# An FFT mixing and relu-squared feed-forward kernel: the first block by eight plain products, w_out's sums moved to VectorE, another order of roundings and G

## The chip, the cores and the metric

One core of a Trainium2 chip. The time is device microseconds of the whole program, the median of several runs. The profile's span (first to last instruction) is about 1.8 us shorter than the time. Engines: TensorE (PE, its weight loads PEld), VectorE (DVE), ScalarE (ACT), GpSimd (POOL); SP issues the transfers.

## The reference, cut to what matters

```python
x: (8, 3008, 256)                      # batch, sequence, width; float32
X = np.fft.fft(np.fft.fft(x, axis=1), axis=2).real        # attention part
h = X.reshape(24064, 256) @ w_in       # w_in (256, 2048), float64 in memory
g = np.maximum(h, 0.0) ** 2
out = g @ w_out                        # w_out (2048, 256), float64 in memory
```

## The kernel before: the parts that matter

The two transforms never appear as such. Of the sequence transform three small arrays P, Q and E are made (cosine and sine sums, in groups called `dft_ops` with table products `pd` and VectorE's joins); the transform over the width is multiplied into w_in once, which gives G1, G2 and gE. A **step** then handles 128 columns of w_in twice (j and j + 8) for 251 frequencies. Eight steps are a block, six blocks a batch of the sequence, eight batches the whole: 384 steps.

```python
def front(b, k0, n, j, between):       # 4 products, 6 VectorE instructions
    for h in range(2):
        ...
        nc.tensor.matmul(hP, G1[:, fs], pt[:, ks], ...)             # ph
        nc.tensor.matmul(hQ, G2[:, fs], qt[:, ks], ...)             # ph
        nc.vector.scalar_tensor_tensor(out=t, in0=et[:, ks], ... in1=hP, ...)   # he
        tt(out=g[:, h, 0, 0:n], in0=t, in1=hQ, op=ALU.add)
        tt(out=g[:, h, 1, 0:n][:, ::-1], in0=t, in1=hQ, op=ALU.subtract)
        between()                      # a piece of the next batch's transform
def combine(n, g):                     # ScalarE, then GpSimd
    act(v, v, AF.Relu); act(v, v, AF.Square)
    gt(out=s1, ...); gt(out=s2, ...); gt(out=s3, ...); gt(out=s4, ...)
def back(n, j, g, s, final):           # 7 products with sums in place of 8
    products = [("mA", 0, wout[:, j, 0, 0], g[:, 0, 0]), ... ("mD", 0, wout[:, j, 1, 1], s[:, 3])]
```

The seven products are a Strassen scheme: they need four sums of g in every step (GpSimd) and, once, four sums of w_out's quarters.

The first block has a second task. The weights lie in memory as 64-bit floats and are rounded by hand, one piece (128 x 512) at a time: two VectorE instructions and three on ScalarE start it, three on VectorE end it.

```python
def convert(dst, src):
    ...                                                  # transfer of the raw words
    nc.vector.tensor_scalar(out=eb, in0=high, ...)       # start: exponent bits
    act(e, eb, AF.Relu, ...); act(eb, e, AF.Relu, ...)
    nc.vector.tensor_scalar(out=mb, in0=high, ...)       # start: mantissa bits
    act(rest, low, AF.Copy, scale=2.0 ** -32)
    def finish():                                        # end
        nc.vector.scalar_tensor_tensor(out=eb, ...)
        tt(out=m, in0=mb, in1=rest, op=ALU.add)
        nc.vector.scalar_tensor_tensor(out=dst, in0=pairs(m), ..., in1=pairs(e), ...)
    return finish
def load_win(j):  ... finish(); then G1, G2, gE of j: products pg, pe and three ScalarE copies
def load_wout(j): ... finish(); then four GpSimd sums of w_out's quarters
...
for i in range(len(steps) + LAG + 4):                    # LAG = 2
    if i < NJ:
        for _ in range(2 if i + 2 < NJ else 1):
            next_weight()              # starts one piece, ends the one started before it
    g = front(b, k0, n, j, between)
    ... back() of step i - 2 ...
    flight.append(((b, k0, n, j), g, combine(n, g)))
```

## Time and profile before

| | before |
|---|---|
| time, median of 3 (range) | 2010.53 us (2009.85 to 2014.74) |
| span of the profiled run, granted clock | 2008.3 us, 0.990 |
| TensorE busy | 1959.6 us |
| first `ph` / first `he` | 67.79 / 69.16 us |
| `ph` of step 8 (second block) | 132.28 us |
| first `ph` of batch 1 | 341.55 us |

How to read it: TensorE is the bound, so only its idle time can be won without taking products away. The three marks in the last rows cut the run into pieces that can be compared one by one: the transform of batch 0, the first block, the rest of batch 0 (210 us), and seven batches that the change does not touch. One more line, from who waited for whom between 60 and 120 us (total, number, longest, in us):

```profile
PE pg L236 <- DVE win L220: 17.3, 6, 4.5
```

All waits of TensorE in that stretch are of this one kind, for the last instruction of a rounding of w_in.

### The profile page before, as it was taken

How to read it: one execution, taken by the hardware profiler on the slowest of the kernel's cores; microseconds unless marked ns; L12 is line 12 of the kernel's file. 1: busy time of each engine (PE TensorE's matmuls, PEld its weight loads, DVE VectorE, ACT ScalarE, POOL GpSimd, SP SyncE). 2: the span in 40 equal slices, each digit the busy share in tenths (PEclk: the TensorE clock that was granted, in tenths of full speed). 3: DMA queues.
4: the chain of work that ended last, by engine and by line, in shares of the span. 5: the costliest groups of instructions: out<-in, count | busy, mean ns of one | idle time of the engine just before them, and what ended most of it. 6: DMA issues, size and time to landing. Idle time of an engine off the chain costs nothing.

```text
span 2008.3 us, 27310 instructions
## 1 busy us (share of the span) xinstructions
PE 1959.6 (98%) x9088; PEld 1702.4 (85%) x9088; DVE 1395.1 (69%) x3463; ACT 897.9 (45%) x973; POOL 1199.8 (60%) x1763
## 2 busy tenths in 40 slices
PE   5799999999999999999999999999999999999998
PEld 3578888888888888888888888888888888888887
DVE  6899766877577765787557875687757776555554
ACT  1554444444444544444444444444444444444443
POOL 0366655766566665666556665566656675556664
PEclk8899999999999999999999999999999999999999
DMA  6223101110011101111011110111001100100100
GB/s 182 85 63 61 30 11 32 35 44 22 11 37 47 27 22 30 33 31 43 16 26 37 35 33 11 31 38 41 22 11 40 44 11 16 31 11 11 21 11 21
DMA packets 144687, 68.49 MB, mean 34 GB/s; under 512 B 128440, under 2 KB 135547, under 8 KB 144546
## 3 DMA queue, kind: packets, MB, share of 16 engines
q1 hardware_dynamic: 143470, 66.24, 14.1%
q8 instruction: 71, 1.16, 0.2%
q10 hardware_dynamic: 1076, 0.52, 0.1%
q14 instruction: 70, 0.57, 0.1%
HBM read 42.03 MB, written 24.68 MB: 33 GB/s over the span
## 4 chain that ended last, share of the span: by engine, by line
PE 95%; DVE 3%; DMA 1%; issue 0%; ACT 0%; SPq 0%; DVEq 0%
PE ph L413 16%; PE mA L456 16%; PE mC L456 16%; PE ph L414 16%; PE mB L456 16%; PE mD L456 8%; PE pd L353 5%; PE pg L236 1%; DMA xt<-in_x_dram 1%; DVE he L416 0%; DMA raw<-in_moe_w_in_dram 0%; DVE fd L217 0%; DVE fs L219 0%; DVE g L419 0%; DVE win L220 0%
## 5 line engine op out<-in xcount | busy, mean ns | idle before, releaser
L427 ACT ACTIVATE g<-g 128x1004 f32<-128x1004 f32 (+1 forms) x384 | 399.5, 1040 | 883.0 <-DVE g L419 506.1
L416 DVE SCALAR_TENSOR_TENSOR he<-Et,gE,ph 128x251 f32<-128x251 f32 (+1 forms) x768 | 361.7, 471 | 480.9 <-PE ph L414 479.5
L433 POOL TENSOR_TENSOR s<-g 128x251 f32<-128x251 f32 (+1 forms) x384 | 253.4, 660 | 629.2 <-ACT g L428 569.1
L413 PE MATMUL ph<-Pt,G 128*128 128x251 f32 (+1 forms) x1536 | 452.6, 375 | 0.9 <-DVE g L419 0.9
L414 PE MATMUL ph<-Qt,G 127*128 127x251 f32 (+1 forms) x1536 | 451.2, 374 | 0.0
L428 ACT ACTIVATE g<-g 128x1004 f32<-128x1004 f32 (+1 forms) x384 | 399.3, 1040 | 12.2
L456 PE MATMUL mA<-g,wout 128*128 128x251 f32 (+1 forms) x1536 | 389.5, 375 | 0.0
L456 PE MATMUL mC<-s,wsum 128*128 128x251 f32 (+1 forms) x1536 | 389.3, 374 | 0.0
L418 DVE TENSOR_TENSOR g<-he,ph 128x251 f32<-128x251 f32 (+1 forms) x768 | 320.6, 417 | 56.0 <-ACT g L428 0.5
L456 PEld LDWEIGHTS mA<-g,wout 128*128 128x128 f32 x1536 | 288.3, 189 | 43.5 <-issue 4.0
L413 PEld LDWEIGHTS ph<-Pt,G 128*128 128x128 f32 x1536 | 287.7, 189 | 42.9 <-issue 3.2
L414 PEld LDWEIGHTS ph<-Qt,G 127*128 127x128 f32 x1536 | 291.2, 190 | 35.8
L456 PEld LDWEIGHTS mC<-s,wsum 128*128 128x128 f32 x1536 | 291.6, 190 | 35.2
L419 DVE TENSOR_TENSOR g<-he,ph 128x251 f32<-128x251 f32 (+1 forms) x768 | 314.1, 409 | 0.0
L434 POOL TENSOR_TENSOR s<-s,g 128x251 f32<-128x251 f32 (+1 forms) x384 | 286.8, 747 | 30.1
L435 POOL TENSOR_TENSOR s<-g 128x251 f32<-128x251 f32 (+1 forms) x384 | 298.1, 776 | 0.0
L436 POOL TENSOR_TENSOR s<-g,s 128x251 f32<-128x251 f32 (+1 forms) x384 | 252.4, 657 | 0.0
L456 PE MATMUL mB<-g,wsum 128*128 128x251 f32 (+1 forms) x768 | 225.1, 374 | 0.0
L456 PE MATMUL mD<-s,wout 128*128 128x251 f32 (+1 forms) x768 | 225.0, 374 | 0.0
L456 PE MATMUL mB<-s,wout 128*128 128x251 f32 (+1 forms) x768 | 224.6, 374 | 0.0
L456 PEld LDWEIGHTS mB<-g,wsum 128*128 128x128 f32 x768 | 145.6, 190 | 17.7
L456 PEld LDWEIGHTS mD<-s,wout 128*128 128x128 f32 x768 | 144.9, 189 | 18.1
(79 smaller groups left out, 1239.9 us busy)
## 6 DMA issues: line engine op xcount, KB each, us to landing
out_dram<-os SPq DMA_DIRECT2D x376, 56.0 KB
xt<-in_x_dram SPq DMA_DIRECT2D x24, 512.0 KB
xt<-in_x_dram SPq DMA_DIRECT2D x16, 384.0 KB
Et<-e_dram SPq DMA_DIRECT2D x7, 752.5 KB
out_dram<-os SPq DMA_DIRECT2D x288, 6.8 KB
raw<-in_moe_w_in_dram SPq DMA_DIRECT2D x16, 256.0 KB
raw<-in_moe_w_out_dram SPq DMA_DIRECT2D x16, 256.0 KB
xt<-in_x_dram SPq DMA_DIRECT2D x8, 480.0 KB
```

The lines of the kernel that those rows point to most:

```text
L413: nc.tensor.matmul(hP, G1[:, fs], pt[:, ks], start=True, stop=True)
L414: nc.tensor.matmul(hQ, G2[:, fs], qt[:, ks], start=True, stop=True)
L416: nc.vector.scalar_tensor_tensor(out=t, in0=et[:, ks], scalar=gE[:, fc:fc + 1], in1=hP, op0=ALU.mult, op1=ALU.add)
L418: tt(out=g[:, h, 0, 0:n], in0=t, in1=hQ, op=ALU.add)
L419: tt(out=g[:, h, 1, 0:n][:, ::-1], in0=t, in1=hQ, op=ALU.subtract)
L427: act(v, v, AF.Relu)
L428: act(v, v, AF.Square)
L433: gt(out=s1, in0=g21, in1=g22, op=ALU.add)
L434: gt(out=s2, in0=s1, in1=g11, op=ALU.subtract)
L435: gt(out=s3, in0=g11, in1=g21, op=ALU.subtract)
L436: gt(out=s4, in0=g12, in1=s2, op=ALU.subtract)
L456: nc.tensor.matmul(acc[nm][:, i, 0:n], w, v[:, 0:n], start=j == 0 and i == 0, stop=j == NJ - 1, skip_group_check=True)
```

## The change

Its intent is to start the steady state earlier. The first block does without sums (eight plain products), so GpSimd is silent while VectorE rounds; w_out's sums are made by VectorE in the second block, when the roundings are over; batch 0's side work starts a block later to leave room for that; G's products are issued a step after their rounding; w_out is rounded before w_in; a rounding is put into a wait in Q's transform; and w_out's halves are separated by reading every second element, not by writing apart.

```diff
-    def pairs(w):
-        return w.rearrange("p c (e h) -> p (c e) h", h=2)
+    def parts(w, k):
+        return w.rearrange("p c (e h) -> p h (c e)", h=k)
...
-            gt = nc.gpsimd.tensor_tensor
-            gt(out=t3, in0=b22, in1=b12, op=ALU.subtract)
+    def sum_wout(j):
+        tt(out=t3, in0=b22, in1=b12, op=ALU.subtract)
...                                              # and three more sums
-    def combine(n, g):
+    def combine(n, g, plain):
...
+        if plain:
+            return None
...
+        if s is None:
+            for c in range(2):
+                for h in range(2):
+                    for side, nm in enumerate(("mA", "mB")):
+                        nc.tensor.matmul(acc[nm][:, h, 0:n], wout[:, j, h, c], g[:, c, side, 0:n], ...)
...
+        weights.append(lambda j=j: load_wout(j))
         if j + 2 < NJ:
             weights.append(lambda j=j: load_win(j + 2))
-        weights.append(lambda j=j: load_wout(j))
...
+    groups_at(20, 25)
     begun = weights.pop(0)()
-    groups_at(16, 20, 17, 18, 19, 21, 22, 23)
-    next_weight()
+    groups_at(21, 22, 23)
+    products = next_weight()
+    groups_at(26, 27, 28, 24, 29)
+    products = [products]
...
-        if i < NJ:
+        if i < 2 * NJ:                           # no side work yet
             return
...
-            if i < NJ:
-                for _ in range(2 if i + 2 < NJ else 1):
-                    next_weight()
...
             g = front(b, k0, n, j, between)
+            if i < NJ:
+                s = combine(n, g, True)
+            elif i < 2 * NJ:
+                sum_wout(j)
...                                              # back() of step i - 2
+        for f in products:
+            f()
+        products = [next_weight() for _ in range(2 if i + 2 < NJ else 1 if i < NJ else 0)]
```

More of the change, by code (lines that the diff above doesn't have):

```diff
@@ L180, in pair_out @@
         return moe_w_out.rearrange("(c j p) (o e) -> j c p o e", j=NJ, p=P, o=1)[j]
-    def pairs(w):
-        return w.rearrange("p c (e h) -> p (c e) h", h=2)
+    def parts(w, k):
+        return w.rearrange("p c (e h) -> p h (c e)", h=k)
     raws = 0
     def convert(dst, src):
+        k = dst.shape[1]
         nonlocal raws
@@ L194, in convert @@
                 nc.sync.dma_start(out=w[:, c].rearrange("p (o e) -> p o e", o=src.shape[2]), in_=src[c])
-            return lambda: nc.vector.tensor_copy(dst, pairs(w))
+            return lambda: nc.vector.tensor_copy(dst, parts(w, k))
         pool, tag = (xp, "x") if raws % (NX + 1) else (ep, "c")
@@ L219, in finish @@
             tt(out=m, in0=mb, in1=rest, op=ALU.add)
-            nc.vector.scalar_tensor_tensor(out=dst, in0=pairs(m), scalar=2.0 ** -20, in1=pairs(e),
+            nc.vector.scalar_tensor_tensor(out=dst, in0=parts(m, k), scalar=2.0 ** -20, in1=parts(e, k),
                                            op0=ALU.mult, op1=ALU.mult)
@@ L228, in load_win, with products @@
         w = ep.tile([P, 2, CH], F32, name="win", tag="sB" if j % 2 else "sA")
-        finish = convert(pairs(w), pair_in(j))
-        def then():
-            finish()
+        finish = convert(parts(w, 1), pair_in(j))
+        def products():
             for tab, G, n in ((cosd, G1, P), (sind, G2, P - 1)):
@@ L244, in then @@
             nc.scalar.copy(gE[:, j::NJ], ps[:, 0:2])
-        return then
+        return finish, products
     def load_wout(j):
-        finish = convert(wout[:, j].rearrange("p h c e -> p (c e) h"), pair_out(j))
-        def then():
-            finish()
-            b11, b12, b21, b22 = (wout[:, j, h, c] for c in range(2) for h in range(2))
-            t2, t3, t4 = (wsum[:, i, j] for i in range(3))
-            gt = nc.gpsimd.tensor_tensor
-            gt(out=t3, in0=b22, in1=b12, op=ALU.subtract)
-            gt(out=b12, in0=b12, in1=b11, op=ALU.subtract)
-            gt(out=t2, in0=b22, in1=b12, op=ALU.subtract)
-            gt(out=t4, in0=t2, in1=b21, op=ALU.subtract)
-        return then
+        return convert(wout[:, j].rearrange("p h c e -> p h (c e)"), pair_out(j)), lambda: None
+    def sum_wout(j):
+        b11, b12, b21, b22 = (wout[:, j, h, c] for c in range(2) for h in range(2))
+        t2, t3, t4 = (wsum[:, i, j] for i in range(3))
+        tt(out=t3, in0=b22, in1=b12, op=ALU.subtract)
+        tt(out=b12, in0=b12, in1=b11, op=ALU.subtract)
+        tt(out=t2, in0=b22, in1=b12, op=ALU.subtract)
+        tt(out=t4, in0=t2, in1=b21, op=ALU.subtract)
     folded = {}
@@ L382, in odd_n, with join_1 @@
             def odd_n():
-                ps = psd.tile([P, 512], F32, name="pd", tag="d")[0:n, 0:n0]
-                product(ps, 3)
+                st["odd"] = psd.tile([P, 512], F32, name="pd", tag="d")[0:n, 0:n0]
+                product(st["odd"], 3)
+            def join_1():
                 dst = e_rows if b is None else PQE[b][which]
                 nh = S // 8
-                both(dst[:, kp:kp + 2 * n0 - 1:2], dst[:, M - kp - 2 * (nh - 1):M - kp + 1:2], st["c"], ps)
-            return [(0.5, even_n), (0.5, join_4), (0.7, join_2), (1.2, odd_n)]
+                both(dst[:, kp:kp + 2 * n0 - 1:2], dst[:, M - kp - 2 * (nh - 1):M - kp + 1:2], st["c"],
+                     st["odd"])
+            return [(0.5, even_n), (0.5, join_4), (0.7, join_2), (0.0, odd_n), (1.2, join_1)]
         ops = [] if b is None else [(0.0, start)]
@@ L445, in back @@
                 acc[nm] = psm.tile([P, 2, CH], F32, name=nm, tag=nm)
+        if s is None:
+            for c in range(2):
+                for h in range(2):
+                    for side, nm in enumerate(("mA", "mB")):
+                        nc.tensor.matmul(acc[nm][:, h, 0:n], wout[:, j, h, c], g[:, c, side, 0:n],
+                                         start=j == c == h == 0, stop=j == NJ - 1 and c == 1, skip_group_check=True)
+            return
         products = [("mA", 0, wout[:, j, 0, 0], g[:, 0, 0]),
@@ L457, in back, with gather @@
                              skip_group_check=True)
-    def gather(n, final):
+    def gather(n, plain, final):
         mA, mB, mC, mD = (acc[nm] for nm in ("mA", "mB", "mC", "mD"))
+        if plain:
+            c = ep.tile([P, 2, 2, CK], F32, name="c", tag="c")
+            for side, m in enumerate((mA, mB)):
+                nc.scalar.copy(c[:, side, :, 0:n], m[:, :, 0:n])
+            return c
         sA = ep.tile([P, 2, CK], F32, name="sA", tag="sA")
@@ L527 @@
     for j in range(NJ):
+        weights.append(lambda j=j: load_wout(j))
         if j + 2 < NJ:
             weights.append(lambda j=j: load_win(j + 2))
-        weights.append(lambda j=j: load_wout(j))
     def next_weight():
         nonlocal begun
-        then, begun = begun, weights.pop(0)() if weights else None
-        then()
+        (finish, products), begun = begun, weights.pop(0)() if weights else None
+        finish()
+        return products
     pieces = [[f for _, f in fold(0, t)] for t in range(NT)]
@@ L559 @@
     for_p(0)
-    begun()
+    finish, products = begun
+    finish()
+    products()
     for t in range(1, 4):
         for_p(t)
-    groups_at(0, 4)
+    groups_at(0, 5)
     for_p(4)
@@ L566 @@
     for_p(5)
-    groups_at(5, 6)
+    groups_at(6, 7)
     for_p(6)
+    groups_at(3)
     for n, t in enumerate((4, 5, 6, 0, 1, 2, 3)):
         for_q(t)
-        groups_at(*((3, 7), (8,), (9, 10), (11, 12), (13, 14), (15,), ())[n])
+        groups_at(*((4, 8, 9), (10,), (11, 12), (13, 14, 15), (16, 17), (18,), (19,))[n])
+    groups_at(20, 25)
     begun = weights.pop(0)()
-    groups_at(16, 20, 17, 18, 19, 21, 22, 23)
-    next_weight()
+    groups_at(21, 22, 23)
+    products = next_weight()
+    groups_at(26, 27, 28, 24, 29)
+    products = [products]
     LAG = 2
@@ L606 @@
                 side = ahead(b + 1) if b + 1 < B else []
-                spent, pace = 0.0, sum(t for t, _ in side) / (2 * (per - (0 if i else NJ)) - 6)
+                spent, pace = 0.0, sum(t for t, _ in side) / (2 * (per - (0 if i else 2 * NJ)) - 6)
             g = front(b, k0, n, j, between)
+            if i < NJ:
+                s = combine(n, g, True)
+            elif i < 2 * NJ:
+                sum_wout(j)
         while finished and finished[0][0] <= i:
@@ L615 @@
             if at[3] == NJ - 1:
-                c_ = gather(at[2], final)
+                c_ = gather(at[2], s_ is None, final)
                 finished += [(i + 2 + s, *at[:3], s, c_, final) for s in range(2)]
+        for f in products:
+            f()
+        products = [next_weight() for _ in range(2 if i + 2 < NJ else 1 if i < NJ else 0)]
         if i < len(steps):
-            flight.append(((b, k0, n, j), g, combine(n, g)))
+            flight.append(((b, k0, n, j), g, s if i < NJ else combine(n, g, False)))
 _INS = ['x', 'moe_w_in', 'moe_w_out', 'cos_s', 'sin_s', 'cos_d', 'sin_d', 'alt_d']
```

## The prediction

> **What bounds the kernel now.** I read the page first. TensorE is busy nearly everywhere except at the start: in the row of 40 slices (50 us each) its first two digits are 5 and 7, and every slice from the third to the last but one is 9.
>
> ```profile
> PE 1959.6 (98%) x9088; PEld 1702.4 (85%) x9088; DVE 1395.1 (69%) x3463; ACT 897.9 (45%) x973; POOL 1199.8 (60%) x1763
> PE   5799999999999999999999999999999999999998
> DVE  6899766877577765787557875687757776555554
> ```
>
> All that any change of order can win is the idle time, 2008.3 - 1959.6 = 49 us (2.4%), and it lies in the first 123 us. Second I asked who TensorE waited for after 132 us. Two waits, 1.4 us in 1876 us:
>
> ```profile
> PE ph L413 <- DVE g L419: 0.9, 1, 0.9
> PE po L500 <- DVE c L478: 0.5, 1, 0.5
> ```
>
> Third, the table of stretches. The first block (eight steps j; each loads and rounds one piece of w_in and one of w_out) begins with the first `ph` product at 67.8 us. Two of its steps, then stretches at full work, two from batch 0 (which also folds batch 1) and one from batch 1:
>
> ```profile
> 78.54:88.99 10.45, 6.19 (x27) 5.01 (x26) 9.66 (x17) 6.79 (x11) 5.36 (x8) 0.84 0.31 101
> 109.27:118.19 8.92, 7.57 (x41) 6.50 (x40) 8.09 (x16) 6.69 (x11) 4.76 (x8) 1.00 0.19 59
> 132.00:170.00 38.00, 37.13 (x175) 32.50 (x174) 34.55 (x80) 17.81 (x18) 28.69 (x43) 1.00 0.48 49
> 170.00:208.00 38.00, 37.98 (x178) 33.17 (x177) 34.39 (x83) 17.70 (x18) 26.80 (x37) 1.00 0.20 53
> 345.00:400.00 55.00, 55.00 (x261) 48.95 (x260) 44.16 (x109) 27.08 (x28) 38.61 (x56) 1.00 0.14 35
> ```
>
> A step of the first block takes 8.8 to 11.4 us, VectorE works over 90% of it and TensorE 60 to 85%. A step later takes 11 products of 0.425 us = 4.675 us (the starts of successive steps' products in TensorE's timeline). Fourth, the chain that ended last, over one such step:
>
> ```profile
> 82.76 0.60 DVE fd L217
> 83.36 0.61 DVE fs L219
> 83.99 0.70 DVE win L220
> 84.74 3.60 PE pg L236 x8
> 88.34 0.79 PE pe L242 x8
> 89.12 0.53 PE ph L413 x2
> 89.66 0.44 PE ph L414 x2
> 90.12 0.48 DVE he L416
> ```
>
> VectorE rounds w_in, TensorE at once makes G from it and the step's `ph`, VectorE takes up `ph`: nothing is prepared a step ahead. Meanwhile VectorE rounds w_out, beside GpSimd's sums, which stretches it. In VectorE's timeline:
>
> ```profile
> 82.34 0.42 DVE L212 TENSOR_SCALAR fs<-raw 128x512 uint32<-128x512 uint32 x1
> 82.67 0.68 DVE L217 SCALAR_TENSOR_TENSOR fd<-raw,fd 128x512 uint32<-128x512 uint32 x1
> 83.99 0.69 DVE L220 SCALAR_TENSOR_TENSOR win<-fs,fd 128x512 f32<-128x512 f32 x1
> 85.38 0.94 DVE L212 TENSOR_SCALAR fs<-raw 128x512 uint32<-128x512 uint32 x1
> 86.24 1.20 DVE L217 SCALAR_TENSOR_TENSOR fd<-raw,fd 128x512 uint32<-128x512 uint32 x1
> 68.24 1.08 DVE L220 SCALAR_TENSOR_TENSOR wout<-fs,fd 128x512 f32<-128x512 f32 x1
> ```
>
> The same instruction takes 0.42 or 0.94 us, 0.68 or 1.20, without or with GpSimd reading beside it. The w_out form of L220 takes 1.08 us even with GpSimd still idle (its first sum starts at 69.41).
>
> [...] L220 for w_out now writes with jumps of a whole part of the tile; changed, it writes densely and reads every second element. [...] after 4.26 us idle at 84.74 the first four `pg` take 1.87 us to the next group's start, against 0.96 at 95.19 (1.28 us idle). [...]
>
> **The change part by part.**
>
> *1. Before the first block.* Q's odd product no longer is followed at once by its join; the rounding of win1 fills VectorE's 4.22 us wait there (49.86 to 54.08), and four roundings that used to lie between Q's end (58.3) and the first `he` (69.2), 10.8 us in all, no longer do. My walk: the last fold of Q ends 0.9 us earlier (45.3, one join put behind it), the even products until about 48, Q's odd products about 48 to 52 and 53 to 56.5 (the second waits for win1's rounding and join_2 on VectorE; part of both at half clock), first `ph` at about 57.5 instead of 67.8, first `he` at T0 = 58.5 instead of 69.2.
>
> *2. A step of the first block.* VectorE, without GpSimd beside it: six front instructions 2.33 us (79.67 to 82.00), start of a rounding 0.68 (twice), end of a rounding 1.93 (twice): 7.55 us. Before, the same list took 9.7 to 10.5. TensorE: 4 + 8 products of 0.425 = 5.1, plus G of the next step 1.84 + 0.8 = 2.65: 7.75 us. But ScalarE is in the loop in program order: Relu and Square of g (each 1.07), G's two copies and gE (0.68), and only then the two Relus for the next w_in (1.46), without which L217 can't go on. From a step's first `he`: 2.45 + 2.14 + 0.68 + 1.46 = 6.7 us until L217 may start, where VectorE would be ready at 5.6; then 1.93 for the rounding: next `he` at 8.65 us. So about 8.65 us a step, 1.1 of it VectorE waiting for ScalarE, and TensorE 90% busy with gaps under 1 us[...]. L220's saving of 0.39 disappears in that wait.
> Six such steps: 51.9 us. Step 6 has one start and one end, and TensorE's order gives about 5.75. TensorE then ends `ph` of step 7 and the products of step 5 at T0 + 51.9 + 9.95, and begins `ph` of step 8 at 58.5 + 61.85 = 120.4 us. Before: 132.28 us. Won: 11.9 us.
>
> *3. The eighth product.* 8 steps x 0.425 = 3.4 us more TensorE work. Six of these are in the stretch counted in 2; steps 6 and 7 come after: +0.85 us. GpSimd's 32 sums of g and 32 of w_out (2.8 + 1.9 us busy a step) are off the path.
>
> *4. Second block.* VectorE takes w_out's sums: 4 x 8 of 128x128, estimated from its joins of 95 and 189 columns (0.25 and 0.35 us, 0.17 and 0.27 start to start) at 0.2 each start to start, at most 0.4 with GpSimd beside: 0.8 to 1.6 a step over 2.33, under 4.675. Two steps of lag remain before they are needed. Nothing lost. Its 0.9 us wait at 147.4 goes.
>
> *5. Blocks three to six of batch 0.* The side work (folds of batch 1, its transforms, the column sums: nominal 7 x 3.5 + 6 x 2.9 + 7 x 0.6 = 46.1) is spread over 2 x 32 - 6 = 58 half-steps instead of 74: 0.795 instead of 0.623 each; batch 1 spreads 36.1 over 90, 0.40. VectorE's busy share at 0.623 is (34.55 + 34.39)/76 = 0.907 of a 2.34 us half-step, 2.12 us; at 0.40 it is 44.16/55 = 0.803, 1.88. Linear through both, 0.795 gives 2.31 of 2.34 us. It just fits over the folds; for moments that don't I put 0 to 4 us, centre 1.2.
>
> Sum: 2010.5 - 11.9 + 0.85 + 1.2 = 2000.7, say 2001 us.
>
> **The rivals.**
> (a) *VectorE or TensorE alone sets the first block.* At 7.75 us a step the six steps take 5.4 us less: about 1995.5. For it: ScalarE works only 6.8 us a step. Against: its order above.
> (b) *A full VectorE in blocks three to six.* [...] an average at 99% leaves bursts that `ph`'s two buffers can't take up. If TensorE waits 0.2 us in each of 31 fold half-steps, 6 us come back: 2006. For it: 91% today already made one wait of 0.9. Against: only one.
> (c) *Nothing won.* If the first block is bound by the number of roundings whatever their order, only 3.4 us of products are added: 2014. Against: GpSimd's visible stretching, and 10.5 us between steps where VectorE's unstretched list is 7.55.
> (d) *Half clock in the first block.* [...] six steps x up to 1 us on the path, 2005 to 2007.
>
> **Range and chances.** The start (part 1) is good to 1.5 us, a step of the first block to 0.5 us (3 in six), the crowding to 2. Together about 4 to 5: 1996 to 2007. 2% is 40 us, nearly all idle time of TensorE, while Q's transform and the loads stay: no path leads there. Nor does one lead to 40 us more. Faster 0.01, same 0.98, slower 0.01.
>
> **What would show it.** Right: first `ph` at about 57.5 us; steps of about 8.65 us in the first block; L207, L212, L217 there at 0.42 and 0.69 throughout; L220 for w_out at 0.69; a wait of L217 for ScalarE of about 1 us a step; `ph` of step 8 near 120; TensorE's waits after that together under 4 us, its busy time about 3.4 us up less what full clock saves. Wrong: steps over 10 us, waits of L413 for VectorE through blocks three to six, or the first `ph` after 62 us.

The sum came to 2000.7, put as 2001 us. A step of 8.65 us counts TensorE at full clock: that was the author's assumption. L220's saving of 0.39 us is 1.08 us less the 0.69 of the w_in form; that the w_out form would come down to it was an estimate (the trace after shows 0.69 us). Rival (d) goes by the kernel before at 104.94 us: after a wait of 2.20 us the granted clock was 0.53 up to 108.60, and G with `pe` took 4.33 us up to `ph`, against 2.64 at 95.19 after a wait of 1.28 us, at a granted clock of 1.00. Half clock in part 1: the granted clock of the kernel before was 0.74 from 40 to 60 us.

## The result, and the profile after

| | before | after | after, again | predicted |
|---|---|---|---|---|
| time, median (range) | 2010.19 us (2008.45 to 2014.74) | 2000.04 us (1997.33 to 2001.55) | 1999.70 us (1997.53 to 2000.94) | 2001 (1996 to 2007) |
| ratio to before, 95% interval | | 0.9945, 0.9924 to 0.9965 | 0.9947, 0.9934 to 0.9959 | within 2% |
| first `ph` / first `he` | 67.79 / 69.16 | 56.21 / 57.78 | 55.22 / 56.74 | 57.5 / 58.5 |
| step of the first block, full clock | 8.8 to 8.9 | 8.50 | 8.50 | 8.65 |
| `ph` of step 8 | 132.28 | 121.92 | 118.50 | 120.4 |
| batch 1's first `ph` minus that | 209.27 | 210.41 | 210.40 | 211.3 |
| TensorE busy (profiled run) | 1959.6 | 1963.1 | 1959.4 | + 3.4, less what full clock saves |

"After, again" is the same kernel run once more among the experiments below, with five runs.

Only what lies before batch 1 changed. From batch 1's first `ph` to the end it is 2008.3 - 341.55 = 1666.8 us before and 1999.2 - 332.33 = 1666.9 us after. The balance of the profiled runs: 10.36 us earlier at step 8, 1.14 us given back in the rest of batch 0, 9.1 us of span.

The page of the changed kernel, to be held against the first fence of the prediction:

```profile
PE 1963.1 (98%) x9104; PEld 1704.3 (85%) x9104; DVE 1392.0 (70%) x3492; ACT 897.6 (45%) x973; POOL 1159.3 (58%) x1695
PE   6899999999999999999999999999999999999998
POOL 0026645666566755676556665666656675566664
```

TensorE's busy time is 3.5 us up (in the repetition it is not, 1959.4 us: it also holds what half clock adds, up to 2.07 us for four products of G in place of 1.02, see below); its first two slices rise from 5 and 7 to 6 and 8. GpSimd is now silent until the third slice. Now three steps of the first block, in the table of stretches (length, then busy time and instructions of PE, PEld, DVE, ACT and POOL, then the granted clock, the share of the transfer engines and GB/s):

```profile
66.30:76.43 10.13, 8.83 (x25) 7.45 (x26) 7.58 (x18) 6.68 (x12) 0.00 (x0) 0.53 0.31 104
86.32:94.83 8.51, 8.02 (x41) 6.88 (x40) 7.58 (x18) 6.51 (x12) 0.00 (x0) 1.00 0.39 123
94.83:103.34 8.51, 8.02 (x42) 6.94 (x41) 7.58 (x18) 6.50 (x12) 0.00 (x0) 1.00 0.38 124
```

VectorE's list is 7.58 us in every step (9.66 in the step shown of before), and no step is as short as that: it waits 0.9 us. Where, the chain that ended last tells, for the step from 86.32 us, after its front part (start, length, what):

```profile
88.76 1.05 ACT g L427
...
89.83 1.04 ACT g L428
90.88 0.53 ACT G L237 x2
91.41 0.07 ACT gE L244
91.48 0.63 ACT fd L210
...
92.13 0.73 ACT fd L211
...
92.89 0.69 DVE fd L218
93.58 0.61 DVE fs L220
...
94.22 0.69 DVE win L221
94.91 0.40 DVE he L415
```

Before, this chain went rounding, G's products on TensorE, `ph`, `he`. Now TensorE has left it: Relu and Square of the step's g, G's copies and the next piece's two Relus follow one another on ScalarE, and VectorE's rounding waits for the last of them. VectorE's timeline shows the wait and the durations:

```profile
90.64 0.69 DVE L221 SCALAR_TENSOR_TENSOR wout<-fs,fd 128x512 f32<-128x512 f32 x1
91.71 0.42 DVE L213 TENSOR_SCALAR fs<-raw 128x512 uint32<-128x512 uint32 x1
92.89 0.69 DVE L218 SCALAR_TENSOR_TENSOR fd<-raw,fd 128x512 uint32<-128x512 uint32 x1 [0.76 <-ACT fd L211]
```

The roundings are unstretched, w_out's last instruction takes 0.69 us (1.08 before), and 0.76 us pass for ScalarE's L211.

The step from 66.30 to 76.43 is not like the others: granted clock 0.53. TensorE's timeline says why:

```profile
67.60 2.07 PE L236 MATMUL pg<-win,cosd 128*128 128x256 f32 x4 [2.97 <-DVE g L418]
```

In the first two steps there are no `back` products yet, so TensorE waits 2.97 us for VectorE and then works at half clock; it shows in this step and the next (10.13 and 9.89 us instead of 8.5). The end of the wait, the time at half clock and what follows, in the table of stretches:

```profile
64.64:66.94 2.30, 0.00 (x0) 0.00 (x0) 2.23 (x5) 2.15 (x4) 0.00 (x0) 1.00 0.09 34
66.94:77.18 10.24, 9.58 (x27) 8.03 (x28) 7.69 (x17) 6.69 (x11) 0.00 (x0) 0.50 0.31 104
77.18:86.32 9.14, 9.14 (x48) 8.22 (x47) 6.87 (x15) 6.28 (x11) 0.00 (x0) 1.00 0.36 116
```

The length of a wait alone does not tell what follows. After 2.25 us in experiment 6 the next four products of G took 2.07 us; after 2.24 us in experiment 5 they took 1.13. What decides it was not tested.

Five profiled runs of kernels whose instructions are the same up to step 8 (this one, its repetition and three experiments that change only later blocks) all waited 2.96 or 2.97 us there and had products at half clock after it: in two of them the eight `pe` that follow G took 0.95 us again, in three they still took 1.71. From first `ph` to `ph` of step 8 the two took 63.3 and 63.4 us, the three 64.6, and 65.7 and 65.7 us. Their first `ph` lay at 55.1 to 57.7 us and `ph` of step 8 at 118.5, 119.3, 119.7, 121.9 and 123.3 us. So a difference of two or three microseconds in the total can't be told from one profile; below, steps at full clock are compared, and medians only where they differ by more.

In the second block and the rest of batch 0, TensorE's only wait, and VectorE's busy time in the stretch where the folds are densest:

```profile
PE ph L412 <- DVE g L418: 0.9, 1, 0.9
```

```profile
165.00:203.00 38.00, 38.00 (x180) 33.41 (x179) 35.83 (x92) 17.98 (x19) 27.62 (x36) 1.00 0.23 62
```

One wait of 0.9 us, as before the change, with VectorE at 94%.

### The profile page after: what moved, and what is told of

It is laid out like the page before. It is cut to its first block, busy times and chain, and to the rows that moved or that the text cites. A ratio compares the mean times of both kernels' runs of the same rounds, so it can differ in the third digit from the quotient of the medians.

```text
span 1999.2 us, 27284 instructions
## 1 busy us (share of the span) xinstructions
PE 1963.1 (98%) x9104; PEld 1704.3 (85%) x9104; DVE 1392.0 (70%) x3492; ACT 897.6 (45%) x973; POOL 1159.3 (58%) x1695
## 4 chain that ended last, share of the span: by engine, by line
PE 94%; DVE 3%; ACT 1%; DMA 1%; issue 0%; SPq 0%; DVEq 0%; ACTq 0%
PE ph L412 16%; PE ph L413 16%; PE mA L465 16%; PE mC L465 16%; PE mB L465 16%; PE mD L465 8%; PE pd L349 5%; DMA xt<-in_x_dram 1%; DVE he L415 0%; PE mA L452 0%; PE mB L452 0%; DVE g L418 0%; PE pg L236 0%; DVE fd L301 0%; ACT g L427 0%
## 5 line engine op out<-in xcount | busy, mean ns | idle before, releaser
L435 POOL TENSOR_TENSOR s<-g 128x251 f32<-128x251 f32 (+1 forms) x376 | 248.6, 661 | 746.5 <-ACT g L428 690.9
L465 PE MATMUL mC<-s,wsum 128*128 128x251 f32 (+1 forms) x1504 | 381.3, 374 | 0.0
L465 PE MATMUL mA<-g,wout 128*128 128x251 f32 (+1 forms) x1504 | 380.9, 375 | 0.0
L465 PEld LDWEIGHTS mA<-g,wout 128*128 128x128 f32 x1504 | 282.5, 189 | 41.6 <-issue 2.9
L465 PEld LDWEIGHTS mC<-s,wsum 128*128 128x128 f32 x1504 | 285.5, 190 | 34.5
L436 POOL TENSOR_TENSOR s<-s,g 128x251 f32<-128x251 f32 (+1 forms) x376 | 282.1, 750 | 29.4
L437 POOL TENSOR_TENSOR s<-g 128x251 f32<-128x251 f32 (+1 forms) x376 | 290.3, 772 | 0.0
L438 POOL TENSOR_TENSOR s<-g,s 128x251 f32<-128x251 f32 (+1 forms) x376 | 247.9, 659 | 0.0
L465 PE MATMUL mB<-g,wsum 128*128 128x251 f32 (+1 forms) x752 | 220.4, 374 | 0.0
L465 PE MATMUL mD<-s,wout 128*128 128x251 f32 (+1 forms) x752 | 220.3, 374 | 0.0
L465 PE MATMUL mB<-s,wout 128*128 128x251 f32 (+1 forms) x752 | 219.9, 374 | 0.0
```

The lines of the kernel that those rows point to most:

```text
L435: gt(out=s1, in0=g21, in1=g22, op=ALU.add)
L436: gt(out=s2, in0=s1, in1=g11, op=ALU.subtract)
L437: gt(out=s3, in0=g11, in1=g21, op=ALU.subtract)
L438: gt(out=s4, in0=g12, in1=s2, op=ALU.subtract)
L465: nc.tensor.matmul(acc[nm][:, i, 0:n], w, v[:, 0:n], start=j == 0 and i == 0, stop=j == NJ - 1, skip_group_check=True)
```

## The experiments

Each is the changed kernel with one thing different. Times are compared by the ratio to the kernel before, run in the same rounds; 0.001 is 2 us. The changed kernel stands at 0.9947 (its repetition). The theory is: the first block's step is set by VectorE and ScalarE together (the chain above), GpSimd's sums had stretched it (0.42 us to 0.94 and 0.68 to 1.20 in the trace before), and the later issue of G takes TensorE out of it. The rivals are in each expectation.

### 1. The order ahead of the first block undone

```diff
...                                              # the same for the groups before these
-    groups_at(21, 22, 23)
-    products = next_weight()
-    groups_at(26, 27, 28, 24, 29)
+    groups_at(20, 25, 21, 22, 23, 24, 26, 27, 28, 29)   # every join right after its product
+    products = next_weight()                            # win1's rounding last
```

> The changed kernel with the order of before ahead of the first block: each odd product of the transforms is followed at once by its join, and win1 is rounded after Q's last join. In the changed kernel the first ph begins at 56.2 us, the first he at 57.8, ph of step 8 at 121.9. Theory (filling VectorE's wait in Q's transform is worth about the length of one rounding, 1.93 us plus a start of 0.68, because the rounding else stands between Q's last join and the first he): first he at about 61, ph of step 8 at about 125, total about 3 us above the changed kernel. Rival (the first block absorbs it, as TensorE waits there anyway): ph of step 8 within 1 us of 121.9 and the total unchanged.

Measured: 2002.36 us, ratio 0.9958 (0.9941 to 0.9975). First `he` at 59.74 us, against 56.6 to 59.2 (mean 57.6) in the five profiles of the changed order. It follows the first `ph` by 3.73 us, in the five by 1.52 to 1.57 us. `ph` of step 8 came at 121.44 us: that is the rival's sign (within 1 us of 121.9), but it is worth little, as the five range from 118.5 to 123.3. The first step took 9.13 us, with half clock after a wait of 2.68 us (G's second four products took 1.63 us and `pe` 1.71, in the next step 1.13 and 0.95), the others 8.50. Against the repetition of the changed kernel, which had one slow step of 9.19, step 8 is 2.9 us late; against the first profile it is 0.5 early. So the rounding in Q's wait brings the first `he` forward by about 2 us, less than the expected 3, and the gain in the total is not resolved: the intervals overlap. Inconclusive on the total.

### 2. Seven products and GpSimd's sums back in the first block

```diff
-        return convert(...), lambda: None
+        finish = convert(...)
+        def then():
+            finish()
+            sum_wout(j)                # on GpSimd, in the first block
+        return then, lambda: None
...
-                s = combine(n, g, True)
-            elif i < 2 * NJ:
-                sum_wout(j)
+                s = combine(n, g, False)
```

> The changed kernel, but the first block by the seven products again, with GpSimd's sums of g and of w_out in it as before; order and layout of roundings as changed. TensorE has 8 x 0.425 = 3.4 us less to do. Theory (GpSimd's reads stretch the roundings, which are on the path): the roundings show 0.9 and 1.2 us again in place of 0.42 and 0.69; VectorE's list of 7.55 us a step grows by 1 to 2 us, and past the 0.76 us that it waits for ScalarE; steps of 9 to 10 us, ph of step 8 at 124 to 129, total 2 to 6 us above the changed kernel. Rival (the order alone made the gain, and the stretching fits into the wait): steps stay 8.5 us, ph of step 8 at about 121 or before, total 1 to 3 us below the changed kernel.

Measured: 2003.82 us, ratio 0.9965 (0.9950 to 0.9980), 3.6 us over the changed kernel although TensorE has 3.4 us less to do. Steps of 9.6 to 9.7 us at full clock, `ph` of step 8 at 127.32. Two instructions of its VectorE timeline, and one of its steps:

```profile
103.95 0.94 DVE L213 TENSOR_SCALAR fs<-raw 128x512 uint32<-128x512 uint32 x1
104.87 1.16 DVE L218 SCALAR_TENSOR_TENSOR fd<-raw,fd 128x512 uint32<-128x512 uint32 x1
```

```profile
98.18:107.86 9.68, 7.93 (x39) 6.48 (x38) 9.44 (x17) 6.51 (x11) 6.06 (x9) 1.00 0.33 108
```

VectorE's list is 9.44 instead of 7.58 us for the same 17 or so instructions, and in these steps no wait for ScalarE is left. In the same step GpSimd is idle until 102.94 us, and the same two instructions of w_out's rounding, from 100.90 us, take 0.42 and 0.69 us. The theory holds: GpSimd's sums cost 1.9 us a step (9.44 - 7.58); the wait of 0.76 us swallows part, and the step grows by 1.2. The rival, that the stretch would fit into the wait, falls. It is the steps that show it: the interval of the total touches those of the changed kernel (up to 0.9959 and 0.9965).

### 3. G's products right after the rounding, in the new order

```diff
         finish()
-        return products
+        products()
+        return lambda: None
```

> The changed kernel, but G's products follow at once on the rounding of w_in, as before, not a step later. Theory (the step ahead is what takes TensorE's G and ph off the loop): after the rounding VectorE waits for G's products (2.65 us, or 3.6 at half clock) and ph (0.85) before its next he; ScalarE's copies fall away ahead of the two Relus, -0.68. Steps of 11 to 12.5 us in place of 8.5, six of them, so ph of step 8 at 137 to 146 and a total of about 15 to 22 us above the changed kernel. Rival (the roundings without GpSimd are the gain, and order is a detail): steps under 9.5 us, total within 4 us of the changed kernel.

Measured: 2029.43 us, ratio 1.0091 (1.0076 to 1.0106): 29 us over the changed kernel, slower than the kernel before. Steps of 13.5 to 14.7 us. VectorE at the head of a step:

```profile
114.41 0.48 DVE L415 SCALAR_TENSOR_TENSOR he<-Et,gE,ph 128x251 f32<-128x251 f32 x1 [5.51 <-PE ph L413]
```

In TensorE's queue `ph` stands behind G (G from 108.95 us, `ph` from 113.28), and G waits for the rounding that is VectorE's last work of the step. The direction was expected, the size too small: 3.6 us were counted for G at half clock and 0.85 for `ph`. G with `pe` took 4.33 us, since `pe` (0.8 us) had been left out, and from `ph` to `he` it was 1.13. After TensorE's waits of 3.82 to 7.22 us there was half clock in every step (four products of G in 1.63 to 2.08 us, and the next four in 1.62 to 1.91, against 1.02 at full clock). It isolates the issue of G only for this order of pieces; experiment 9 undoes both.

### 4. w_out written in pairs as before

```diff
-    ... rearrange("p h c e -> p h (c e)"), pair_out(j))
+    ... rearrange("p h c e -> p (c e) h"), pair_out(j))     # and read in pairs
```

> The changed kernel with w_out's last rounding instruction writing in pairs as before (1.08 us in place of 0.69). Theory (VectorE waits 0.76 us a step for ScalarE, so 0.39 more of VectorE's work is hidden): the wait shrinks to about 0.37, steps stay at 8.5 us, ph of step 8 within 1 us of 121.9, total unchanged. Rival (VectorE's list sets the step): steps of 8.9 us, ph of step 8 about 2.5 us later, total 2 to 3 us longer.

Measured: 1998.39 us, ratio 0.9938 (0.9923 to 0.9953), the changed kernel's time; steps at full clock of 8.50 us. `ph` of step 8 came at 118.19 us, not within 1 us of 121.9 as expected, but beside the repetition's 118.50, with half clock for about as long in both (the first four of G in 2.08 and 2.07 us, `pe` in 0.95 again). Two instructions:

```profile
95.43 1.07 DVE L223 SCALAR_TENSOR_TENSOR wout<-fs,fd 128x512 f32<-128x512 f32 x1
97.67 0.69 DVE L220 SCALAR_TENSOR_TENSOR fd<-raw,fd 128x512 uint32<-128x512 uint32 x1 [0.38 <-ACT fd L213]
```

The instruction is 0.38 us longer and the wait for ScalarE 0.38 us shorter (0.76 before). The layout buys nothing in this kernel; it shows that VectorE's own list does not set the step.

### 5. ScalarE's part of the rounding issued before the step's front

```diff
+            if i + 1 < NJ:
+                start_weight()         # VectorE's two instructions, ScalarE's three
             g = front(b, k0, n, j, between)
...
-        products = [next_weight() for _ in range(2 if i + 2 < NJ else 1 if i < NJ else 0)]
+        products = []
+        if i < NJ:
+            finish_weight()
+        if i + 2 < NJ:
+            start_weight()
+            products = [finish_weight()]
```

> The changed kernel, but in each step of the first block the start of win(i+2)'s rounding (two VectorE instructions, and with it ScalarE's three) is issued before the step's front part, so ScalarE's work for it comes ahead of Relu and Square of g. Theory (the step of 8.5 us is set by the loop over ScalarE: Relu, Square, G's copies, then the two Relus of the next w_in): VectorE's wait of 0.76 us for ScalarE goes, steps come to about 7.75 us (TensorE's own list) or 7.6 (VectorE's); six steps win 4 to 5 us, ph of step 8 at 117 to 118. Rival (TensorE's order and its two psum buffers set the step): steps stay at 8.5 us, total unchanged.

Measured: 1993.22 us, ratio 0.9910 (0.9894 to 0.9927), 7 us under the changed kernel. Steps of 7.78 us, `ph` of step 8 at 114.40. One step:

```profile
80.98:88.76 7.78, 7.78 (x42) 7.01 (x41) 7.57 (x17) 6.62 (x12) 0.00 (x0) 1.00 0.41 136
```

TensorE is busy for the whole 7.78 us and VectorE has no gap in its timeline either; the wait for ScalarE is gone. The theory holds, and the gain is above what it said (4 to 5): six steps of 0.72 us are 4.3, and the profiled run had no step at half clock, which is worth up to 3 more (the 3.0 us it cost the changed kernel's first profile). After TensorE's remaining wait in the second step, 2.24 us, G's products took 1.13 us for four; in experiment 6 they took 2.07 after 2.25 us. The two lines, experiment 5 first:

```profile
66.72 1.13 PE L236 MATMUL pg<-win,cosd 128*128 128x256 f32 x4 [2.24 <-DVE g L418]
67.86 2.07 PE L236 MATMUL pg<-win,cosd 128*128 128x256 f32 x4 [2.25 <-DVE g L418]
```

Whether its other runs were as lucky, no profile shows. This is the fastest kernel, though not told apart from experiment 6.

### 6. The same, with one more rounding moved into Q's wait

```diff
-    groups_at(26, 27, 28, 24, 29)
+    groups_at(26, 27, 28, 24)
+    start_weight()
+    finish_weight()
+    groups_at(29)
```

> As the run with the early start, and in addition w_out's first rounding goes into VectorE's remaining wait in Q's transform (3.37 us before the last odd product's join), so that all roundings are one ahead. Theory (VectorE's list is 7.6 us a step and TensorE's 7.75, and TensorE's wait of 2.97 us at 64.6 with the half clock after it comes from VectorE's two roundings in step 0): one rounding of 2.6 us leaves the first block altogether, the half clock goes, ph of step 8 at 111 to 114, total 8 to 11 us below the changed kernel, about 1990. Rival (the first join of Q is late then, or TensorE's psum buffers set the steps): total at best equal to the run with the early start alone.

Measured: 1994.13 us, ratio 0.9916 (0.9901 to 0.9931): no better than experiment 5. A miss. Each step still holds two roundings, so the `he` of successive steps still lie 7.78 us apart for five steps, and TensorE's wait of 2.25 us in the second step stays as well. The half clock, which was to go, came after it (the first four products of G in 2.07 us, the next four in 1.70, `pe` in 0.95 again), without delaying a `he`. The rounding that left is missed only in steps 6 and 7, where TensorE sets the pace anyway. Moving a chain by one place does not shorten it.

### 7. Batch 0's side work squeezed into three blocks, and spread over five

Two runs, to test how near VectorE is to its limit:

```diff
-        if i < 2 * NJ:                 # (0 if i else 2 * NJ) in the pace as well
+        if i < 3 * NJ:                 # first run; 1 * NJ in the second
```

> The changed kernel with batch 0's side work begun one block later still (third block empty, 42 half-steps, 1.10 nominal us each instead of 0.795). A test of how near VectorE is to its limit. Theory (linear in the side work, from the trace before: 2.12 us a half-step at 0.623 and 1.88 at 0.40, so 2.63 at 1.10, over the 2.34 of TensorE): TensorE waits in some 22 half-steps for VectorE, 4 to 8 us in all; first ph of batch 1 at 336 to 340 in place of 332.3. Rival (VectorE's stretching gives way, TensorE hides it): waits under 2 us.

Measured: 2006.38 us, ratio 0.9980 (0.9965 to 0.9994). Batch 1 begins 336.92 - 119.33 = 217.6 us after step 8, 7.2 us more than in the changed kernel. TensorE's waits after 125 us:

```profile
PE ph L412 <- DVE g L418: 7.7, 6, 2.2
```

That is the theory's 4 to 8 us: with 1.10 nominal us of side work per half-step VectorE is full at times. But the theory had some 22 short waits; there were six, up to 2.2 us. So the sum came out right, not the way it spreads.

> The changed kernel with batch 0's side work begun with the second block as before (74 half-steps, 0.623), while VectorE also makes w_out's sums there. Theory (the delay of the side work is needed: 2.12 us a half-step plus 0.65 to 1.2 for the sums is over 2.34): TensorE waits 4 to 9 us in the second block, then no more. Rival (two steps of lag and the buffers take it up, so the delay of the side work was not needed): waits under 1.5 us, total equal to the changed kernel.

Measured: 2001.15 us, ratio 0.9953 (0.9938 to 0.9968). TensorE waits three times for VectorE between 148 and 166 us, 2.6 us in all; batch 1 begins 212.1 us after step 8, 1.7 us more than in the changed kernel. So the delay of the side work is worth 1.7 us: more than the rival's nothing, less than half of the theory's least. The likely reason, not tested: I had added VectorE's averages and left out that `front` of one step may run while TensorE still works off `back` of an earlier one.

### 8. w_out's sums by GpSimd in the second block

```diff
     def sum_wout(j):
+        tt = nc.gpsimd.tensor_tensor
```

> The changed kernel with w_out's four sums per step of the second block on GpSimd instead of VectorE. GpSimd's list there: sums of g 2.84 us and sums of w_out 4 x 0.53 = 2.1, 4.95 us a step against 4.675 of TensorE. Theory (VectorE was the right place): GpSimd falls behind by 0.3 us a step, 2.2 us in eight[...], and TensorE waits 0 to 3 us. Rival (two steps of lag take it up): no wait, total equal to the changed kernel within 1 us; first ph of batch 1 minus ph of step 8 stays 210.4 us.

Measured: 1998.65 us, ratio 0.9942 (0.9927 to 0.9958); batch 1 begins 211.3 us after step 8, 0.9 us more, and TensorE waits 1.4 instead of 0.9 us. In time nothing; in the trace under a microsecond. What matters is that the sums left the first block, not which engine makes them in the second.

### 9. The order of before inside the first block, without GpSimd

```diff
-        weights.append(lambda j=j: load_wout(j))
         if j + 2 < NJ:
             weights.append(lambda j=j: load_win(j + 2))
+        weights.append(lambda j=j: load_wout(j))
...
+            if i < NJ:
+                for _ in range(2 if i + 2 < NJ else 1):
+                    next_weight()()    # G's products at once
             g = front(b, k0, n, j, between)
```

> The changed kernel (eight plain products, dense layout, Q's order) with the order of before inside the first block: w_in is rounded before w_out, two roundings ahead of each front part, and G's products stand in TensorE's queue at once after the rounding, so the rounding of w_out lies beside them. It tells what the order of the first block is worth without GpSimd. Theory (the new order is worth a few us): first he about 8 us later (66 to 67), with three more roundings done by then; steps of 8.6 us at full clock to 9.6 at half clock; ph of step 8 at 121 to 127 and a total 0 to 6 us above the changed kernel. Rival 1 (order is the main gain): steps of 10.5 us as before, ph of step 8 after 129. Rival 2 (order is worth nothing): ph of step 8 at or before 121.9.

Measured: 2005.83 us (2003.36 to 2009.59), ratio 0.9980 (0.9966 to 0.9993), 6.6 us over the changed kernel. First `he` at 62.5 us (expected 66 to 67, with three more roundings done by then; the trace has two), two steps of 10.5 us (9.6 expected at half clock) with TensorE waiting 4.25 us and working at half clock after it (G's second four products took 1.91 us both times, against 1.03 in the later steps), the rest 8.85 us; `ph` of step 8 at 124.35. With w_out's rounding beside G, the old order loses only 0.35 us a step at full clock. What it loses more lies in the two steps with the waits of 4.25 us and half clock after them, and its runs scatter by 6 us. The theory (0 to 6 us) is met at its edge, passed by 0.6.

### 10. The changed kernel again

> The changed kernel itself once more, beside the two others of this call. If the half clock at the start falls by chance (three runs of the same instructions showed ph of step 8 at 119.3, 121.9 and 123.3 us), its median stays at 2000 within 2 us, and its ratio to the kernel before at 0.9945 within 0.0015; the first-block steps at full clock are 8.50 us again, and the number of steps at half clock may differ.

Measured: 1999.70 us, ratio 0.9947 (0.9934 to 0.9959); steps of 8.50 us at full clock, one at 9.19. As expected.

## Why the prediction was right

The time, 2000.04 us (1999.70 on repetition), against 2001 predicted. By the prediction's own steps:

1. **Before the first block.** First `ph` 57.5 predicted, 56.21 measured; first `he` 58.5 and 57.78. Right within the stated 1.5 us. But "four roundings" between Q's end and the first `he` was miscounted: three end there (the last instructions of L220 begin at 60.26, 62.98 and 68.24 us), and a wait of 2.44 us for ScalarE is part of the 10.8. VectorE makes the same sixteen roundings; one went into Q's wait, and two now come after the first `he`. Experiment 1 puts the wait's worth at about 2 us at the first `he`.
2. **A step of the first block.** VectorE's list 7.55 predicted, 7.58 measured; L218 free to start 6.7 us after `he` predicted, 6.6 measured (94.83 to 101.40); the step 8.65 predicted, 8.50 measured; the wait for ScalarE 1.1 predicted, 0.76 measured. The mechanism, ScalarE's place in the chain, is shown from both sides: 0.38 us more on VectorE disappear in the wait (experiment 4), and ScalarE's work issued earlier makes steps of 7.78 us (experiment 5). L221 for w_out at 0.69 us was right and, as said, worth nothing; the trace before already held a like case, L217, which reads every second word of `raw` at 0.68 us. What step 2 left out is the half clock in the first two or three steps, which had stood among the rivals as (d): TensorE's gap of 2.97 us there is not "under 1 us". It cost 3.0 us in the first profile and 0.7 in the repetition, which is most of the difference between the two: `ph` of step 8 came 1.5 us late in the one and 1.9 early in the other.
3. **The eighth product.** 3.4 us predicted, "less what full clock saves". The busy time rose by 3.5 us in the first profile and fell by 0.2 in the repetition, so it can't measure this term. What shows it is the spacing of steps that hold eight `back` products: 5.10 us, against 4.68 with seven. Steps 8 and 9 are the last two of them, 0.85 us in all: that is most of the 1.14 us by which the rest of batch 0 grew. Right.
4. **Second block.** Nothing lost: right, but the sums were put too low. From start to start they took 0.32 us alone (0.2 predicted) and up to 0.80 beside GpSimd (0.4), so 2.40 us in one step (135.50 to 137.90), not at most 1.6; with the front part's 2.33 that is over a step's 4.675, and no wait followed. The wait of before at 147.4 us went, and another of the same length came at 222.9.
5. **Blocks three to six.** A busy share of 99% and 1.2 us lost were predicted; 94.3% (35.83 of 38 us) and about 0.3 us (1.14 - 0.85) were measured. The line through two points was too steep here, yet at 1.10 nominal us it gave about the right loss (experiment 7, 7.2 us), in fewer and longer waits. Below saturation I would now trust it only as an upper bound.

Two misses in opposite directions, the half clock and the crowding, about cancelled in the first run. That is luck: in the profile of the repetition both went the same way, 1.9 and 0.9 us under. One sentence on the kernel before was wrong: "nothing is prepared a step ahead". The piece rounded at step i belonged to step i + 2 even then; what tied `ph` of step i to it was only that G stood ahead of `ph` in TensorE's queue. Experiments 3 and 9 show what that costs: a great deal if the rounding of w_in is VectorE's last work of the step, little if another rounding lies beside G.

So where do the 10 us come from? With the seven products and GpSimd back, 3.6 us are lost (experiment 2); with the old order, 6.6 (experiment 9). Layout and engine of the sums count for nothing measurable (4 and 8); the later side work is worth 1.7 us of a cost that the change itself brings (7); the order in Q's transform is worth about 2 us at the first `he`, unresolved in the total (1). The two large parts together give the measured 10 us, though parts undone singly need not add up, and half clock is in both (after waits of 4.07 us in experiment 2 and 4.25 in experiment 9).

## What to carry to other kernels

When several engines, each working off its own list, share a warm-up loop, write down for one step which instruction each waits for; the step is set by the longest such circle, often through an engine that is only three quarters busy, and a change to the busiest engine's list may not show at all until that circle is cut (0.38 us more a step vanished in experiment 4). Issue the first part of a slow preparation before the step's main work, on every engine it passes through: here that alone (experiment 5) was worth 7 us more, two thirds of what the whole change had brought. Extra work on the bound engine can pay, if it silences an engine that stretches another one on the path (here 3.4 us of products against 1.9 us a step of VectorE's list, experiment 2).
